# A gated mix of linear attention and a Fourier transform: x's rest rows stored by SyncE, forms stored in halves, x rings of four, low parts ahead of evictions, PE in the text's order

## The chip, the cores and the metric

The kernel runs on one core of one Trainium2 chip. The metric is the device time of one execution in microseconds. Before the change it is 793.74 us, the median of three runs (793.55 to 794.37).

A core has five engines that run their own instruction streams: PE (TensorE, matrix products, with its weight loads as PEld), DVE (VectorE), ACT (ScalarE), POOL (GpSimd) and SP (SyncE, which only issues DMAs here). Sixteen DMA engines move data between DRAM and the on-chip memory. Matrix products write to eight banks of an accumulator memory, from where DVE and ACT read them.

## The reference

```
x = A_x                                     # 2048 rows of 576
g = sigmoid((x * gate_w).sum(-1))           # one gate a row
# a: linear attention, 32 heads of 18
q, k, v = split(x @ wqkv)
pq, pk = phi(q), phi(k)                     # phi(t) = (t + 1 if t > 0 else exp(t)) + 1e-6
kv = pk^T v ; z = pk.sum(rows)              # head by head
a = (pq kv / (pq z + 1e-6)) @ wo
# b: real part of a 2-D Fourier transform, with the matrices given
b = seq_re @ (x @ hid_re^T) - seq_im @ (x @ hid_im^T)
out = g * a + (1 - g) * b
```

Everything is float32. The kernel keeps that precision by splitting each factor of a product into a high part (rounded to the type that PE takes) and a low part (what rounding left), and multiplying high by high, high by low and low by high: three matmuls for one. The high part is made by ACT (`hi_of`, L163), the low part by a subtraction on DVE (`lo_of`, L173).

## The kernel before, in words

The text runs through these stages. From the first k tiles on, ACT and DVE run in the order of the text (`pace`, L168), SP does so throughout (L199); PE's and POOL's order is set by the compiler's scheduler.

1. **k** (L508): for 16 tiles of 128 rows, two halves of 288 columns of k are computed and go through phi into `acc` and `pk`. The transposed x tiles are loaded by SP through a ring of three buffers (`xs_ring`, `load_next`, L240), split by `split_next` (L246).
2. **kv** (L583): 20 steps (five chunks of x's columns times four groups of tiles) form x^T pk; with wv this gives kv. The steps also load wv, wq and wo, and sum z.
3. **q** (L754 to L777): 16 tiles (`q_tile`, L637) give phi(q) in `acc[i]`, and the gate. `build_m` folds kv and wo into one matrix; `normalise` (L653) divides by pq z in parts, called as `go(norms)`.
4. **out** (L1055): each tile is transposed on PE (`transposed`, L681), multiplied by that matrix, scaled by the gate and stored to DRAM (`att`).
5. **hidden run 1** (`Hidden.run`, L849): x @ hid_re^T by a seven-product scheme of the Strassen kind, for eight pairs of row blocks, `p` = 0 to 7. Each product is seven matmuls: six on 512 of the columns and one on the rest rows, which are 32 x 3 rows of all forms in one tile.
6. **sequence 1** (`sequence`, L961): seq_re times the result, again with seven products, in 8 rows of output (`j`) times 4 batches (`b`); each row's seven banks are evicted by DVE (L1020 to L1038) and mixed with `att` (`mix`, L1010) into `mid`.
7. **hidden run 2** and **sequence 2**: the same with hid_im and seq_im, from `mid` to `out`.

For 5 to 7 the operands are prepared earlier as *forms*. A `Left` part (L333) loads quarters of x into SBUF, makes the sums of quarters (`make`, L352), splits them, and stores the seven forms to DRAM (`xm`, 1792 KB for a pair of blocks). Parts 2 to 6 are made during the k and kv stages, one piece a call of `left_part` (L376), which goes on to the next part when one is at its end: pieces are what stands between two `yield`s. The part of x's rest rows (`k` = `NP`) lies at `ACC_AT`, on the memory of `acc[0]` to `acc[6]`, and is stored to `xr` by six DMAs of POOL (L372), whose target is 4 x 32 rows of 3584 bytes. `right` (L382) does the same for the hidden matrices (`wm`).

In a hidden run `load_x` loads two of a pair's seven forms at a time, `load_pair` all in four DMAs, `load_rest` the rest rows (336 KB) and `load_w` one matrix form. `follow` and `follow_rest` (L852) say which pair's loads are issued during and after which pair's products. `Layout` (L89) says which memory they take.

In a sequence, `Matrix.load` fetches batches of seq (`craw`) and `make` (L942) adds forms in three pieces; the third piece first calls `tick()`, which issues the low parts that wait in `pending`, and then makes the high part. At the end of a row that third piece comes only after the first two additions of the eviction (L1022).

Of the kernel before, what the change touches and what calls it, by code (L numbers as in the profile page):

```python
# [8 lines left out]
F = mybir.dt.float32  # L9
# [66 lines left out]

LAY_Q = dict(xs=(-256, 4864, 9984), hi=(15104, 20864), lo=(26688, 31296))

# [10 lines left out]
class Layout:  # L89
# [23 lines left out]
    def rest(self, p):  # L113
        if p == 2 or p == 1 and not self.swap:
            return T_AT + (4 * TPAIR + 7 * XF if p == 2 else 60416)
        return WF_AT + 4 * WF if p % 2 else SLOT_AT + 14 * XF + 3 * WF
# [6 lines left out]
def kernel(  # L123
# [209 lines left out]
    class Left:  # L333
# [18 lines left out]
        def make(self):  # L352

            r, c = self.f[:, :, 1], self.c
            add(r[:, 0], r[:, 1], r[:, 6])
            add(r[:, 4], r[:, 2], r[:, 6], ALU.subtract)
            yield
            add(r[:, 3], r[:, 0], r[:, 2], ALU.subtract)
            add(r[:, 6], r[:, 5], r[:, 3], ALU.subtract)
            yield  # L360
            hi_of(c[:, :4, 0], r[:, :4])
            hi_of(c[:, 4:, 0], r[:, 4:])
            yield
            lo_of(c[:, :4, 1], r[:, :4], c[:, :4, 0])
            yield
            lo_of(c[:, 4:, 1], r[:, 4:], c[:, 4:, 0])
            if self.k < NP:
                nc.gpsimd.dma_start(out=xforms[self.k], in_=c.bitcast(F))
                return
            for j in range(6):  # L370
                k, g = j // 2, j % 2
                nc.gpsimd.dma_start(out=xrest[g, :, k], in_=self.plain.bitcast(F)[:, g, k // 2])  # L372

# [8 lines left out]
    def right(src, rest, order):  # L382
# [10 lines left out]
        def piece(k, start):  # L393

            c = load(k, start)
            r = c.bitcast(F)[:, :, 1]
            yield
            add(r[:, 3], r[:, 5], r[:, 0], ALU.subtract)
            add(r[:, 5], r[:, 2], r[:, 5], ALU.subtract)
            yield  # L400
            add(r[:, 4], r[:, 2], r[:, 3], ALU.subtract)
            add(r[:, 6], r[:, 4], r[:, 1], ALU.subtract)
            yield
            hi_of(c[:, :, 0], r)
            yield
            if k < 2:
                lo_of(c[:, :4, 1], r[:, :4], c[:, :4, 0])
                yield
                lo_of(c[:, 4:, 1], r[:, 4:], c[:, 4:, 0])
                nc.gpsimd.dma_start(out=main[:, :, k], in_=c.bitcast(F))  # L410
            else:
                rows = slice(32, 64)
                lo_of(c[rows, :, 0], r[rows], c[rows, :, 0])
                yield
                nc.gpsimd.dma_start(out=last, in_=c.bitcast(F)[:, :, 0])
# [92 lines left out]
    for i in range(2, NT):  # L508
# [13 lines left out]
        if 8 <= i < 12:  # L522
            xg_load()
        load_next()
        for k, j in enumerate((2, 3, 9, 13)):
# [224 lines left out]
    def m_row(h, j):  # L750
        return mhi[:, j, half(h)] if j <= KC else mlo[:, j - 5, half(h)]

    wr_forms, wr_pieces = right(wr, wr_rest, ((0, T_AT + 60416), (1, T_AT + 76544),
                                              (2, T_AT + 60416)))  # L754
    q_tile(0)
    wo_split.pop(0)()
# [9 lines left out]
    for i in range(4, NT):  # L766
# [3 lines left out]
        for k, j, n in ((0, 4, 2), (0, 5, 1), (0, 6, 2), (1, 4, 1), (1, 7, 2), (1, 8, 1),  # L770
                        (1, 11, 2), (2, 9, 1), (2, 12, 2), (2, 13, 1), (2, 14, 2)):
            if i == j:
                go(wr_pieces[k], n)
        if i in (5, 8, 13, 14, 15):
            go(norms)
        if i in (9, 10):
            split_m(i - 9)  # L777
# [29 lines left out]
    class Hidden:  # L807
# [41 lines left out]
        def run(self, m):  # L849
            rest = None  # L850

            follow, follow_rest = {0: 4, 2: 6, 3: 5, 5: 7}, {0: 4, 1: 3, 3: 5, 4: 6, 5: 7}  # L852
            self.load_pair(3)
            for p in range(NP):
                fs = Factors(T_AT + p * TPAIR)
                factors.append(fs)
                t = fs.raw
                p3, p2, e = (at(y_ring.next(), [P, HALF], F, "y") for _ in range(3))
                be, bx, bg, bf = (bank()[:, :HALF] for _ in range(4))
# [101 lines left out]
    def sequence(m, g, src, dst, last=None, between=None):  # L961
        late, held, stores = [], [], []
        for n in range(NP * NB):
# [21 lines left out]
            if n == 1:  # L985
                while backlog:
                    backlog.pop(0)()
            end = last is not None and j == NP - 1
            held.append((b, c))
# [28 lines left out]

            nc.scalar.activation(c11, ps[1], AF.Copy)
            add(c12, ps[6], c11, ALU.subtract)  # L1020
            add(c11, ps[2], c11)
# [25 lines left out]
    hidden = Hidden(wr_forms, Layout(0))  # L1047
    nxt = transposed(0)
    made = {}
# [5 lines left out]
    for i in range(NT):  # L1055
# [8 lines left out]
        nc.gpsimd.dma_start(out=att[i], in_=acc[i])  # L1064
        go(norms, 2)
        for k, n in plan.get(i, ()):
            go(made[k], n)
# [7 lines left out]
        if i == 7:  # L1075
            hidden.load_rest(0)
        for k, j in enumerate((9, 10, 13, 15, 2, 3, 4)):
            if i == j:
                hidden.load_w(k)
# [15 lines left out]
    def late(n):  # L1095
# [16 lines left out]
        if n == NP * NB - 1:  # L1112
            second.load_w(5)
            second.load_w(6)
            for k in (2, 4, 6):
                second.load_x(1, k)
            second.load_pair(2)
            second.load_rest(2)

    first.run(mr)  # L1120
    sequence(mr, gate_n, att, mid, between=late)
# [91 lines left out]
```

## Time and profile before

| | us |
|---|---|
| median of three runs (range) | 793.74 (793.55 to 794.37) |
| the profiled execution's own time | 789.25 |
| its span, first to last instruction | 787.5 |
| mean granted clock of PE | 0.979 |

The costliest groups of the page, with busy time, mean duration in ns, and the idle time just before them:

```profile
L997 PE MATMUL bank<-fh,c 128*128 128x288 f32 x1792 | 357.2, 295 | 4.6 <-DVE c L173 4.5
...
L163 ACT ACTIVATE c<-craw 128x1792 fp32r<-128x1792 f32 (+1 forms) x84 | 121.2, 1447 | 196.1 <-DVE craw L183 156.4
...
L193 PE MATMUL bank<-wd,xs 128*128 128x288 f32 (+1 forms) x896 | 128.0, 303 | 31.2 <-DVE acc L327 24.3
...
L173 DVE TENSOR_TENSOR c<-craw,c 128x1792 fp32r<-128x1792 f32 (+4 forms) x86 | 142.0, 1653 | 10.1 <-ACT c L163 10.0
...
L846 PE MATMUL bank<-wf,xf 128*128 128x288 f32 x588 | 90.0, 300 | 3.3 <-DMA xf<-xm 1.8
```

A line of the profile names the line of the kernel, the engine, the operation, and the tiles as output<-inputs. L997 is the sequences' matmul, L846 that of the hidden runs, L193 that of k, q and out. `<-` after the bar names what ended most of the idle time. Times in windows and timelines are us from the first instruction of the span.

### The profile page before, as it was taken

Reading aid. Unit: us, or ns where it says so; the run is one execution under the profiler, and the core shown is the slowest. Engines: PE = TensorE matmul, PEld = TensorE weight load, DVE = VectorE, ACT = ScalarE, POOL = GpSimd, SP = SyncE. Lnnn points to the kernel's source line nnn. Section 1 sums busy time; section 2 is a strip of 40 time slices with the busy share of each in tenths; the row PEclk is TensorE's granted clock in tenths of the full one; section 3 lists DMA queues with packets and bytes.
Section 4 is the critical chain, followed back from the end, with each engine's and each line's share of the span. In section 5 each row is a group of like instructions: output and inputs, shape, how many; then the busy total and the mean of one; then the engine's idle time right before and its main releaser. Section 6 shows DMA issues by size and latency. Waiting matters only on the chain.

```text
span 787.5 us, 13817 instructions
## 1 busy us (share of the span) xinstructions
PE 734.8 (93%) x5428; PEld 724.3 (92%) x5428; DVE 599.0 (76%) x993; ACT 332.6 (42%) x518; POOL 54.4 (7%) x92
## 2 busy tenths in 40 slices
PE   7999999339989999999999999999989999999997
PEld 7999999339979999999999999999889999999997
DVE  5769876037898894689889799983678888987775
ACT  6878435227763444344333333320343532332231
POOL 0111210005102121000000000000000000000000
PEclk9999999859999999999999999999999999999999
DMA  4476886216665589955447656868966344454441
GB/s 159 140 258 227 318 269 203 83 28 208 211 205 196 203 287 343 357 171 191 136 127 259 198 187 209 281 211 323 361 239 221 111 141 143 136 169 141 129 148 61
DMA packets 53348, 157.22 MB, mean 200 GB/s; under 512 B 7396, under 2 KB 11940, under 8 KB 52260
## 3 DMA queue, kind: packets, MB, share of 16 engines
q1 hardware_dynamic: 43620, 114.52, 44.2%
q0 software_dynamic: 9376, 41.41, 14.9%
q8 instruction: 43, 0.70, 0.4%
q10 hardware_dynamic: 288, 0.41, 0.1%
q14 instruction: 21, 0.17, 0.1%
HBM read 113.44 MB, written 41.39 MB: 197 GB/s over the span
## 4 chain that ended last, share of the span: by engine, by line
PE 58%; DMA 21%; DVE 9%; issue 7%; ACT 3%; POOL 1%; SPq 0%; DVEq 0%; ACTq 0%; POOLq 0%
PE bank L997 33%; PE bank L193 15%; DMA xf<-xm 7%; PE bank L592 6%; PE bank L846 4%; DMA wm<-wb 3%; DVE c L173 3%; DMA xraw<-in_xa_dram 2%; DMA xr<-xr 2%; DMA craw<-in_xg_dram 2%; DVE craw L183 1%; DVE ys L183 1%; DMA xr<-xb 1%; DVE wb L173 1%; DMA wraw<-in_wo_dram 1%
## 5 line engine op out<-in xcount | busy, mean ns | idle before, releaser
L997 PE MATMUL bank<-fh,c 128*128 128x288 f32 x1792 | 357.2, 295 | 4.6 <-DVE c L173 4.5
L997 PEld LDWEIGHTS bank<-fh,c 128*128 128x128 f32 x1792 | 286.3, 188 | 6.3 <-DVE c L173 5.5
L997 PE MATMUL bank<-fl,c 128*128 128x288 f32 x896 | 253.7, 294 | 0.0
L163 ACT ACTIVATE c<-craw 128x1792 fp32r<-128x1792 f32 (+1 forms) x84 | 121.2, 1447 | 196.1 <-DVE craw L183 156.4
L997 PEld LDWEIGHTS bank<-fl,c 128*128 128x128 f32 x896 | 168.6, 188 | 0.0
L193 PE MATMUL bank<-wd,xs 128*128 128x288 f32 (+1 forms) x896 | 128.0, 303 | 31.2 <-DVE acc L327 24.3
L193 PEld LDWEIGHTS bank<-wd,xs 128*128 128x128 f32 x896 | 123.7, 194 | 34.3 <-DVE acc L327 24.6
L173 DVE TENSOR_TENSOR c<-craw,c 128x1792 fp32r<-128x1792 f32 (+4 forms) x86 | 142.0, 1653 | 10.1 <-ACT c L163 10.0
L183 DVE TENSOR_TENSOR craw<-craw 128x256 f32<-128x256 f32 (+1 forms) x192 | 98.0, 512 | 6.6 <-DMA craw<-in_cr_dram 1.5
L846 PE MATMUL bank<-wf,xf 128*128 128x288 f32 x588 | 90.0, 300 | 3.3 <-DMA xf<-xm 1.8
L846 PEld LDWEIGHTS bank<-wf,xf 128*128 128x128 f32 x588 | 82.8, 191 | 5.5 <-issue 2.6
L193 PE MATMUL bank<-mw,qs 128*128 128x288 f32 x448 | 65.0, 302 | 1.6 <-ACT qs L163 1.5
L193 PEld LDWEIGHTS bank<-mw,qs 128*128 128x128 f32 x448 | 61.4, 192 | 2.5 <-ACT qs L163 1.8
L592 PE MATMUL bank<-pk,c 128*128 128x288 f32 x448 | 61.8, 296 | 1.7 <-ACT c L163 1.7
L183 DVE TENSOR_TENSOR ys<-bank,ys 128x288 f32<-128x288 f32 x63 | 28.8, 458 | 44.8 <-PE bank L997 37.1
L592 PEld LDWEIGHTS bank<-pk,c 128*128 128x128 f32 x448 | 59.7, 188 | 2.7 <-ACT c L163 2.3
L327 DVE SCALAR_TENSOR_TENSOR acc<-bank,e 128x288 f32<-128x288 f32 x64 | 28.3, 454 | 41.2 <-DMA xr<-xb 27.0
L173 DVE TENSOR_TENSOR fl<-fl,fh 128x864 fp32r<-128x864 f32 (+1 forms) x32 | 34.2, 1093 | 11.2 <-ACT fh L163 9.9
L325 ACT ACTIVATE e<-bank 128x288 f32<-128x288 f32 x64 | 25.6, 400 | 33.3 <-DVE acc L327 24.4
L163 ACT ACTIVATE fh<-fl 128x864 fp32r<-128x864 f32 (+1 forms) x32 | 29.9, 953 | 15.2 <-DVE fl L183 15.2
L173 DVE TENSOR_TENSOR xs<-xraw,xs 128x640 fp32r<-128x640 f32 (+2 forms) x33 | 26.5, 803 | 11.6 <-ACT xs L163 11.5
L1062 ACT ACTIVATE acc<-bank,gate 128x288 f32<-128x288 f32 x32 | 16.0, 501 | 40.1 <-PE bank L193 39.9
(102 smaller groups left out, 618.0 us busy)
## 6 DMA issues: line engine op xcount, KB each, us to landing
xf<-xm SPq DMA_DIRECT2D x42, 512.0 KB, 9.2
craw<-in_cr_dram SPq DMA_DIRECT2D x32, 512.0 KB, 4.0
craw<-in_ci_dram SPq DMA_DIRECT2D x32, 512.0 KB, 3.7
xm<-xb POOLq DMA_DIRECT2D x8, 1792.0 KB, 7.7
xraw<-in_xa_dram SPq DMA_DIRECT2D x31, 320.0 KB, 4.1
wm<-wb POOLq DMA_DIRECT2D x4, 2016.0 KB, 8.6
wf<-wm SPq DMA_DIRECT2D x14, 576.0 KB, 5.4
xr<-xr SPq DMA_DIRECT2D x16, 336.0 KB, 6.1
```

The costliest lines, as they stand in the source:

```text
L163: return nc.scalar.activation(dst, src, AF.Copy, bias=bias)
L173: nc.vector.tensor_tensor(out=dst, in0=src, in1=hi, op=ALU.subtract)
L183: nc.vector.tensor_tensor(out=dst, in0=a, in1=b, op=op)
L193: nc.tensor.matmul(ps, a, b, start=(n == 0), stop=(n == len(pairs) - 1))
L325: nc.scalar.activation(e, ps, AF.Relu, scale=-1.0)
L327: nc.vector.scalar_tensor_tensor(dst, ps, 0.0, e, op0=ALU.max, op1=ALU.add)
L592: nc.tensor.matmul(ps[h][:, :HALF], t[:, a, k], pk[s][:, b, half(h)], start=(s == 0 and n == 0), stop=(s == NT - 1 and n == len(passes) - 1))
L846: nc.tensor.matmul(ps, a, b, start=(start and n == 0), stop=(n == len(ops) - 1), skip_group_check=True)
L997: nc.tensor.matmul(ps[q], c[x][:, l, k], factors[p](y, f), start=(p == 0 and i == 0), stop=(p == NP - 1 and i == 2))
L1062: done.append(nc.scalar.activation(acc[i][:, half(h)], ps[:, :HALF], AF.Copy, scale=gate[:, i:i + 1]))
```

## The change

1. The six stores of x's rest rows are issued by SP, in a piece of their own after the part's last low part.
2. A form is stored in two DMAs, forms 0 to 3 when their low part is made and forms 4 to 6 after theirs (`Left` and `right`); `Left.make` yields after each half, so a part has one more piece.
3. The x ring has four buffers. In the q stage the fourth lies elsewhere; one load more is issued ahead.
4. The pieces of the third `wr` part, the norm parts and the first transposition of the out stage take other places in the q stage; three `load_w` come two tiles later.
5. In the hidden runs the rest rows of pair 3 have memory of their own and are loaded first; `follow` and `follow_rest` are reordered; in run 2 the first pair's three temporaries lie elsewhere; `second.load_rest(2)` comes before the loads of x.
6. In a sequence, `tick()` comes right after the first copy of an eviction; two of the low parts of `backlog` are issued in batch 2 after the adds of the next batch.
7. From the first hidden run on PE too runs in the order of the text.

```diff
@@ Layout.rest
-            if p == 2 or p == 1 and not self.swap:
-                return T_AT + (4 * TPAIR + 7 * XF if p == 2 else 60416)
+            if p == 2:
+                return T_AT + 4 * TPAIR + 7 * XF
+            if p == 3:
+                return T_AT + (NP - 2) * TPAIR + TPAIR // 2
+            if p == 1 and not self.swap:
+                return T_AT + 60416
@@ Left.make
-            lo_of(c[:, :4, 1], r[:, :4], c[:, :4, 0])
-            yield
-            lo_of(c[:, 4:, 1], r[:, 4:], c[:, 4:, 0])
-            if self.k < NP:
-                nc.gpsimd.dma_start(out=xforms[self.k], in_=c.bitcast(F))
-                return
-            for j in range(6):
+            for fs in (slice(0, 4), slice(4, 7)):
+                lo_of(c[:, fs, 1], r[:, fs], c[:, fs, 0])
+                if self.k < NP:
+                    nc.gpsimd.dma_start(out=xforms[self.k][:, fs], in_=c.bitcast(F)[:, fs])
+                yield
+            for j in range(0 if self.k < NP else 6):
                 k, g = j // 2, j % 2
-                nc.gpsimd.dma_start(out=xrest[g, :, k], in_=self.plain.bitcast(F)[:, g, k // 2])
+                nc.sync.dma_start(out=xrest[g, :, k], in_=self.plain.bitcast(F)[:, g, k // 2])
@@ right, piece
-                lo_of(c[:, :4, 1], r[:, :4], c[:, :4, 0])
-                yield
-                lo_of(c[:, 4:, 1], r[:, 4:], c[:, 4:, 0])
-                nc.gpsimd.dma_start(out=main[:, :, k], in_=c.bitcast(F))
+                for fs in (slice(0, 4), slice(4, 7)):
+                    lo_of(c[:, fs, 1], r[:, fs], c[:, fs, 0])
+                    nc.gpsimd.dma_start(out=main[:, fs, k], in_=c.bitcast(F)[:, fs])
+                    if fs.start == 0:
+                        yield
@@ k stage, and ahead of q_tile(0)
-        load_next()
+        if i < NT - 1:
+            load_next()
+        if i == 2:
+            load_next()
...
+    xs_ring.at[3] = T_AT + 105664
+    load_next()
     q_tile(0)
@@ q stage
-                        (1, 11, 2), (2, 9, 1), (2, 12, 2), (2, 13, 1), (2, 14, 2)):
+                        (1, 11, 2), (2, 9, 1), (2, 13, 2), (2, 14, 1)):
...
-        if i in (5, 8, 13, 14, 15):
+        if i in (5, 8, 11, 12, 13):
             go(norms)
+        if i == NT - 3:
+            nxt = transposed(0)
@@ Hidden.run
-            follow, follow_rest = {0: 4, 2: 6, 3: 5, 5: 7}, {0: 4, 1: 3, 3: 5, 4: 6, 5: 7}
+            follow, follow_rest = {0: 4, 2: 5, 3: 6, 5: 7}, {0: 4, 1: 5, 4: 6, 5: 7}
+            self.load_rest(3)
             self.load_pair(3)
...
-                p3, p2, e = (at(y_ring.next(), [P, HALF], F, "y") for _ in range(3))
+                ys = (y_ring.next() for _ in range(3))
+                if p == 0 and self.lay.swap:
+                    o = self.lay.rest(3) + XR
+                    ys = range(o, o + 3 * HALF * 4, HALF * 4)
+                p3, p2, e = (at(o, [P, HALF], F, "y") for o in ys)
@@ sequence
                 while backlog:
                     backlog.pop(0)()
+                rest_lows += pending[-2:]
+                del pending[-2:]
+            elif n == 2:
+                for f in rest_lows:
+                    f()
...
             nc.scalar.activation(c11, ps[1], AF.Copy)
+            tick()
             add(c12, ps[6], c11, ALU.subtract)
@@ out stage
+        if i == 0:
+            go(wr_pieces[2], 2)
...
-        for k, j in enumerate((9, 10, 13, 15, 2, 3, 4)):
+        for k, j in enumerate((9, 10, 13, 15, 4, 5, 6)):
             if i == j:
                 hidden.load_w(k)
@@ late, and ahead of first.run
             second.load_w(6)
+            second.load_rest(2)
             for k in (2, 4, 6):
                 second.load_x(1, k)
             second.load_pair(2)
-            second.load_rest(2)
-
+
+    paced.enter_context(tc.manual_schedule(engines={mybir.EngineType.PE}))
     first.run(mr)
```

More of the change, by code (lines that the diff above doesn't have):

```diff
@@ L74 @@
 QH = HALF, HALF + 2
-LAY_Q = dict(xs=(-256, 4864, 9984), hi=(15104, 20864), lo=(26688, 31296))
+LAY_Q = dict(xs=(-256, 4864, 9984, 43776), hi=(15104, 20864), lo=(26688, 31296))
 PRODUCTS = {1: (4, 0), 6: (2, 4), 2: (6, 1), 5: (1, 3), 7: (0, 5), 3: (3, 2), 4: (5, 6)}
@@ L961, in sequence @@
     def sequence(m, g, src, dst, last=None, between=None):
-        late, held, stores = [], [], []
+        late, held, stores, rest_lows = [], [], [], []
         for n in range(NP * NB):
@@ L1047 @@
     hidden = Hidden(wr_forms, Layout(0))
-    nxt = transposed(0)
     made = {}
```

## The prediction

> **What bounds the kernel now.** I read the page's first two parts first, then the waits of PE, then the timeline of the worst wait, then windows around it.
>
> ```profile
> span 787.5 us, 13817 instructions
> ...
> PE 734.8 (93%) x5428; PEld 724.3 (92%) x5428; DVE 599.0 (76%) x993; ACT 332.6 (42%) x518; POOL 54.4 (7%) x92
> ...
> PEclk9999999859999999999999999999999999999999
> ```
>
> PE is busy for 93% and no other engine comes near, so time is to be had only where PE stands still or runs at half clock. The eighth and ninth digits of the clock row show one such place. The waits of PE (total us, times, longest) name the others:
>
> ```profile
> PE bank L193 <- DVE acc L327: 24.3, 1, 24.3
> PE bank L997 <- DVE c L173: 4.5, 4, 1.4
> ...
> PE bank L846 <- DMA xr<-xr: 4.0, 3, 2.5
> PE bank L846 <- DMA xf<-xm: 1.8, 5, 1.0
> ...
> PE bank L193 <- ACT qs L163: 1.5, 1, 1.5
> PE bank L688 <- DVE acc L666: 1.4, 1, 1.4
> PE bank L193 <- ACT xs L163: 1.4, 3, 0.7
> PE bank L846 <- DVE fl L183: 1.2, 1, 1.2
> ```
>
> One wait is 24.3 of the 40 us listed. The timeline around it (start, length, engine, line; the idle time and its releaser in brackets):
>
> ```profile
> 126.92 6.70 SPq L554 DMA_DIRECT2D wraw<-in_wo_dram  x4
> ...
> 140.14 0.70 POOL L372 DMA_DIRECT2D xr<-xb  x1 [10.05 <-issue]
> ...
> 160.00 0.69 POOL L372 DMA_DIRECT2D xr<-xb  x1 [8.94 <-issue]
> 169.57 0.82 DVE L327 SCALAR_TENSOR_TENSOR acc<-bank,e 128x288 f32<-128x288 f32 x2 [26.95 <-DMA xr<-xb]
> ...
> 170.08 0.85 PE L193 MATMUL bank<-wd,xs 128*128 128x290 f32 x2 [24.33 <-DVE acc L327]
> ```
>
> The buffer of x's rest rows lies on acc. POOL issues its six stores some 10 us apart; the first write of acc (DVE, L327) waits until the sixth, issued at 160.0, has landed, and PE, out of banks, waits for DVE. How wide such a store runs is seen where the sixth is alone on the DMA engines (windows: length, busy of five engines, granted clock, DMA share, GB/s):
>
> ```profile
> 161.20:165.20 4.00, 0.00 (x0) 0.00 (x0) 0.00 (x0) 0.00 (x0) 0.00 (x0) 0.50 0.28 49
> 165.20:169.20 4.00, 0.00 (x0) 0.00 (x0) 0.00 (x0) 0.00 (x0) 0.00 (x0) 0.50 0.17 66
> 161.20:169.20 8.00, 0.00 (x0) 0.00 (x0) 0.00 (x0) 0.00 (x0) 0.00 (x0) 0.50 0.23 58
> 170.10:174.70 4.60, 4.11 (x15) 3.76 (x16) 4.43 (x13) 2.13 (x7) 0.00 (x0) 0.50 0.00 0
> ```
>
> A share of 0.23 of 16 engines is 3.7: the store keeps some four engines busy, at 58 GB/s. The last row is the bill that comes after the wait: 4.6 us at half clock, 2.3 us lost.
>
> **The change part by part.**
>
> *Stores of the rest rows.* The six issues leave POOL for SP; source, destination and the 3.5 KB stretches stay what they were.
>
> ```profile
> xm<-xb POOLq DMA_DIRECT2D x8, 1792.0 KB, 7.7
> ...
> mid<-row SPq DMA_DIRECT2D x16, 288.0 KB, 4.2
> ...
> xr<-xb POOLq DMA_DIRECT2D x6, 448.0 KB, 10.2
> ```
>
> When do they start? `make` now yields once more for each left part, so `left_part` takes five calls for every part where the last call of one used to be the first of the next. Counted through the 12 calls of the k loop and the 20 steps after it, the rest part is made in steps 13 to 17 and stored in step 18, not in step 12. In SP's order that is behind the loads of wo, whose last issue ends at 126.92 + 6.70 = 133.6. So the stores start 26 us later than POOL's first, and gain only if they run more than that much faster. SP's queue does not wait for each to land, so the 10 us pacing goes. What it leaves is the stream: 6 x 448 KB = 2.75 MB. Bounds: at SP's best rate (the 364 GB/s of a window shown below) 7.6 us; at the 49 GB/s of the first window 56 us. I take the row of this very transfer, with its shape: four engines. The first store takes its 8.0 us. The slow start of a single store (49 GB/s at a share of 0.28, 4.5 engines, 11 GB/s each) gives way to 66 GB/s at 0.17, 2.7 engines, 24 GB/s each; four engines with work always queued then move 97 GB/s, 4.7 us a store. The end is 133.6 + 1.2 (issue at 160.0, data by 161.2) + 8.0 + 5 x 4.7 + 0.3 (169.2 to 169.57) = 166.6 against 169.57: **2.9 us gained**, and the half clock stays. Behind the stores on SP wait the loads of x tiles 3 and on; tiles 0 to 2 are in SBUF, so PE has work when acc opens. Step 12's load of wq now waits for the store of form 6, made four steps later than before; I put the delay of c and wv behind it at 2 us (half a form's 7.7 us, less the lead of c), hidden as long as the stores end late.
>
> The Trainium skill, "DMA: Bandwidth & Descriptors", section "Why a DMA increments its semaphore by 16 and not by 1", says that a transfer runs on as many engines as the largest number up to 16 that divides its slowest dimension, whichever engine issues it. It speaks against this change: the slowest dimension is 4 here, and the share of 0.23 agrees for POOL; no row shows SP with it. By that rule the sum stays as it is. The same page, section "Bandwidth", gives 341 GB/s for a load of 1 MB over 128 partitions; by that the six would be over in an estimated 8 us, which is the first rival below.
>
> *Rings of four, q's end.* The three waits on xs (1.4 us in all) go: each x tile is loaded one tile earlier, and SP has idle time there. At the end of the q stage:
>
> ```profile
> 229.11 2.25 DVE L173 TENSOR_TENSOR wb<-wb 32x2016 fp32r<-32x2016 f32 x1
> ...
> 231.40:235.50 4.10, 1.12 (x6) 0.67 (x5) 3.93 (x10) 2.22 (x7) 0.78 (x1) 1.00 0.74 239
> 236.10:239.50 3.40, 3.30 (x15) 3.19 (x14) 3.33 (x8) 0.00 (x0) 0.00 (x0) 0.50 0.28 58
> ```
>
> DVE is full (3.93 of 4.10) while PE stands, and then PE runs 3.4 us at half clock. The change takes that low part (2.25 us) behind the first out tile, moves three norm parts two tiles ahead and tile 0's transposes to tile 13, where PE has two tiles of work split. That removes 1.5 + 1.4 + 1.7 (half of 3.4) = **4.6 us**, with 1.4 for the ring **6.0**. What is late next is the second out tile's low part, behind 2.25 us more on DVE; it has two tiles' time.
>
> *Forms in halves.* Twelve more POOL issues; POOL is busy for 7%: nothing. In the first hidden run the rest of pair 3 now goes into memory that the last form leaves, so SP stands at its start until that form is stored. The old order had that wait a little later:
>
> ```profile
> SPq L938 <- DMA xm<-xb: 5.8, 1, 5.8
> ```
>
> Pairs 0 to 2 are there by then, so PE has 20 us of cover. This run's small waits for xf and xr (0.6 and 0.4 of the 1.8 and 4.0) go: **1.0**.
>
> *Low parts ahead of evictions.*
>
> ```profile
> 371.07 4.56 DVE L173 TENSOR_TENSOR fl<-fl,fh 128x864 fp32r<-128x864 f32 x4
> ...
> 380.21 1.02 DVE L183 TENSOR_TENSOR ys<-bank,ys 128x288 f32<-128x288 f32 x2 [1.55 <-ACT ys L1019]
> 381.15 2.02 DVE L173 TENSOR_TENSOR c<-craw,c 128x1792 fp32r<-128x1792 f32 x1
> ```
>
> DVE stands for 1.55 us until the bank is copied, evicts, and only then makes the low part for which PE waits. With `tick()` before the first add it starts 1.0 to 2.5 us sooner, and every one of the four waits is at most 1.4: 4.5 us go. Banks come free 2 us later; the next row needs the second of them after two products of 6 matmuls, 1.6 us. Against it, two of the four low parts of 4.56 us go behind the next batch's adds, and PE needs the last of them some 0.3 us early in each sequence: 0.6. **3.9 us.**
>
> *Second hidden run, PE in text order.*
>
> ```profile
> 543.05 0.41 ACT L872 ACTIVATE y<-bank 128x288 f32<-128x288 f32 x1 [6.38 <-DVE row L1013]
> ...
> 540.00:560.00 20.00, 18.66 (x138) 18.05 (x137) 12.26 (x25) 6.04 (x12) 0.00 (x0) 1.00 0.98 364
> 560.00:580.00 20.00, 16.12 (x103) 15.03 (x102) 9.69 (x20) 4.14 (x8) 0.00 (x0) 0.91 1.04 359
> ...
> 574.00:577.50 3.50, 3.40 (x14) 3.40 (x15) 2.31 (x4) 1.16 (x3) 0.00 (x0) 0.51 1.04 407
> ...
> 560.01 0.32 SPq L822 DMA_DIRECT2D xr<-xr  x1
> ...
> 569.93 0.80 PE L846 MATMUL bank<-wf,xr 96*128 96x288 f32 x4 [1.09 <-DMA xr<-xr]
> ```
>
> The first product's copy no longer shares a buffer with the sequence's mixes, so the wait of 1.2 goes. For the rest the DMA engines are the wall (shares 0.98 and 1.04). A pair is 49 matmuls, 49 x 18.66 / 138 = 6.6 us of PE, and 1792 + 336 KB = 2.18 MB, 6.0 us of DMA: pairs come hardly faster than they are used. Rests 2 and 3 move forward and no more bytes move. Gone are the waits on xr (1.1 + 2.5) and xf (1.2, what the first run leaves) and half of 3.5 us of clock: 7.7 with the 1.2. New: rest 4 stays behind pair 4 and gets rest 3's 0.9 us in front of it, so it comes at about 570.8, while PE in text order wants it in pair 4's first product, at 540.5 + 4 x 6.6 + 0.9 = 567.8, plus the 0.4 that pair 1 waits for its second load behind rest 2: 2.6 + 0.4 + 0.4 for pair 3's first load. **7.7 - 3.4 = 4.3 us.** Here a gap of 2.6 us might halve the clock again, as the two gaps at 231.4 did (PE busy 1.12 of 4.10). The Trainium skill, "TensorE: Matmul & The Clock Gate", Part 1, puts the window at about 3.4 us, so 2.6 us would leave the clock whole; the trace's 3.0 us in two gaps did not. By the page the term is 4.3, with a halving 2.6; I keep 4.3.
>
> **Sum.** 2.9 + 6.0 + 1.0 + 3.9 + 4.3 = 18.1 us off the profiled span, 769.4 of 787.5. That execution took 789.25 us beside a median of 793.74, so I carry the difference, not the level: 793.74 - 18.1 = **775.6**.
>
> **The rivals.**
> - *SP spreads the stores* as it does its 128-row ones: 7.6 us of stream, acc opens at about 142.7, before PE runs dry at 145.75 (170.08 - 24.33). Then 24.3 + 2.3 go instead of 2.9, less 2 us of the delays in steps 12 to 17, now uncovered: 793.7 - 15.2 - 26.6 + 2 = 754. For it: SP's `mid` stores land in 4.2 us. Against it: the same shape took four engines.
> - *The stores end later than POOL's* (the slower side). If the four engines hamper each other all the time as in the first window, 49 GB/s, the stream takes 56 us and acc opens at 191: 21 us more wait, 793.7 - 15.2 + 21.4 = 800. At the 58 GB/s of a whole store it is 182 and 791. It turns slower than before at a stream of 50 us, 55 GB/s. For it: six starts in six looked alike at 10 us each. Against it: queued engines don't all start together again.
> - *Text order and late loads take back the hidden runs' and sequences' gains*: without 1.0, 3.9 and 4.3 the time is 785. For it: DMA is full there. Against it: the bytes are the same and the rests come sooner.
>
> **How the numbers follow.** Forecast 0.60; spread 0.17; late stores 0.13, half of it slower than before; gains taken back 0.10. Forecast alone: 766 to 783. The range takes in 754 and 58 GB/s: 752 to 791. A measurement here tells about 0.2% from no change: faster by more 0.90, within 0.03, slower 0.07.
>
> **What would show it.** The stores: their issue times on SP (133 to 136), a DMA share near 0.25 after it, and the wait of DVE at L327 ending near 167 (143 or 182 for the rivals). The others: no wait of L688 and L193 near 231, waits of L997 on c under 0.6 in all, no L872 wait on row, and one wait on xr of 2 to 3 us in the second run. I am wrong if SP's issue itself blocks on its four rings and holds back the x tiles, or if acc waits for fewer than all six.

## The result, and the profile after

The changed kernel takes 770.96 us (median of four runs, 767.95 to 771.47) against 794.06 us before (793.55 to 798.15): a ratio of 0.969, 95% interval 0.965 to 0.9731. It is faster, inside the range of 752 to 791, and 4.6 us below the forecast of 775.6. Between the two profiled executions (789.25 and 771.09) lie 18.2 us, by their spans 18.1; by the medians it is 23.1, since the profiled execution of before lay 4.8 us under its median. That sum of 18.1 is what the prediction gave, but not by its terms.

Page of after (compare the span, PE's busy time and the clock row):

```profile
span 769.4 us, 13840 instructions
...
PE 732.4 (95%) x5428; PEld 727.6 (95%) x5428; DVE 600.7 (78%) x993; ACT 336.0 (44%) x518; POOL 56.7 (7%) x98
...
PEclk9999999859999999999999999999999999999999
```

The dent in the clock row is still in the eighth and ninth digits. Waits of PE, after (total us, times, longest):

```profile
PE bank L197 <- DVE acc L331: 19.4, 1, 19.4
...
PE bank L857 <- ACT y L888: 2.4, 2, 1.3
PE bank L857 <- DMA xr<-xr: 2.3, 1, 2.3
PE bank L197 <- ACT zs L167: 1.9, 1, 1.9
PE bank L857 <- DVE fl L187: 1.5, 3, 0.8
```

L197 was L193, L331 was L327, L857 was L846. The wait on acc shrank by 4.9 us. The waits on c, qs, acc L666, xf and on the x tiles of the ring are gone. Two lines are new: y, the copy of a product's bank in a hidden run, and zs, the tile from which z is summed. Waits on fl, a hidden run's result before its low part is made, come three times in place of once.

Where the 18.1 us came from is seen when both executions are cut at the same points: acc's first write after the stall, the first out tile, the first hidden product, the first product of run 2. First before, then after (length of the stretch, PE busy with its matmuls, granted clock, DMA share, GB/s):

```profile
0.00:169.57 169.57, 138.28 (x1008) 0.94 0.60 195
169.57:232.95 63.38, 60.12 (x431) 0.96 0.55 181
232.95:304.04 71.09, 69.53 (x518) 0.98 0.67 234
304.04:540.53 236.49, 232.22 (x1738) 1.00 0.66 224
540.53:787.50 246.97, 234.60 (x1738) 0.99 0.53 174
```

```profile
0.00:164.84 164.84, 138.83 (x1008) 0.94 0.60 202
164.84:226.18 61.34, 60.33 (x430) 0.94 0.57 183
226.18:293.52 67.34, 67.34 (x521) 1.00 0.76 258
293.52:526.97 233.45, 231.92 (x1739) 1.00 0.66 223
526.97:769.40 242.43, 234.01 (x1738) 0.99 0.54 178
```

Acc opens 4.7 us sooner, and this alone counts of all that lies ahead of it, since PE stands there for whatever else comes early or late. Then the stretches gain 2.0 (the rest of q), 3.75 (out), 3.0 (run and sequence 1) and 4.5 us (run and sequence 2): 18.1 with the 4.7, but for rounding. In the out stage PE is now busy for all of its 67.34 us.

### The profile page after: what moved, and what is told of

It is laid out like the page before. It is cut to its first block, busy times and chain, and to the rows that moved or that the text cites. A ratio compares the mean times of both kernels' runs of the same rounds, so it can differ in the third digit from the quotient of the medians.

```text
span 769.4 us, 13840 instructions
## 1 busy us (share of the span) xinstructions
PE 732.4 (95%) x5428; PEld 727.6 (95%) x5428; DVE 600.7 (78%) x993; ACT 336.0 (44%) x518; POOL 56.7 (7%) x98
## 4 chain that ended last, share of the span: by engine, by line
PE 71%; DMA 10%; DVE 2%; SPq 2%; issue 1%; ACT 0%; DVEq 0%; ACTq 0%
PE bank L1018 46%; PE bank L197 16%; PE bank L857 6%; DMA xf<-xm 4%; DMA xr<-xr 2%; DMA xraw<-in_xa_dram 2%; DMA mid<-row 1%; PE bank L695 1%; PE bank L599 1%; SPq L375 1%; DMA wraw<-in_wv_dram 1%; DMA xm<-xb 1%; SPq L247 1%; DVE fl L177 1%; DVE fl L187 0%
## 5 line engine op out<-in xcount | busy, mean ns | idle before, releaser
L1018 PE MATMUL bank<-fl,c 128*128 128x288 f32 x896 | 264.4, 295 | 0.0
L197 PE MATMUL bank<-wd,xs 128*128 128x288 f32 (+1 forms) x896 | 128.1, 305 | 24.7 <-DVE acc L331 19.4
L197 PEld LDWEIGHTS bank<-wd,xs 128*128 128x128 f32 x896 | 125.2, 196 | 26.2 <-DVE acc L331 19.6
L857 PE MATMUL bank<-wf,xf 128*128 128x288 f32 x588 | 93.9, 300 | 4.1 <-ACT y L888 2.4
L857 PEld LDWEIGHTS bank<-wf,xf 128*128 128x128 f32 x588 | 84.8, 191 | 6.0 <-ACT y L888 3.0
L197 PE MATMUL bank<-mw,qs 128*128 128x288 f32 x448 | 63.3, 298 | 0.0
L331 DVE SCALAR_TENSOR_TENSOR acc<-bank,e 128x288 f32<-128x288 f32 x64 | 28.3, 454 | 43.4 <-DMA xraw<-in_xa_dram 23.1
L599 PEld LDWEIGHTS bank<-pk,c 128*128 128x128 f32 x448 | 61.3, 193 | 0.1
L197 PEld LDWEIGHTS bank<-mw,qs 128*128 128x128 f32 x448 | 60.0, 188 | 0.2 <-DVE qs L177 0.2
L857 PE MATMUL bank<-wf,xr 96*128 96x288 f32 x112 | 33.7, 301 | 2.3 <-DMA xr<-xr 2.3
```

Of the source, the lines that this page charges most:

```text
L197: nc.tensor.matmul(ps, a, b, start=(n == 0), stop=(n == len(pairs) - 1))
L331: nc.vector.scalar_tensor_tensor(dst, ps, 0.0, e, op0=ALU.max, op1=ALU.add)
L599: nc.tensor.matmul(ps[h][:, :HALF], t[:, a, k], pk[s][:, b, half(h)], start=(s == 0 and n == 0), stop=(s == NT - 1 and n == len(passes) - 1))
L857: nc.tensor.matmul(ps, a, b, start=(start and n == 0), stop=(n == len(ops) - 1), skip_group_check=True)
L1018: nc.tensor.matmul(ps[q], c[x][:, l, k], factors[p](y, f), start=(p == 0 and i == 0), stop=(p == NP - 1 and i == 2))
```

## The experiments

The line numbers of a run are its own kernel's; they differ by a few from those of after. The times of before beside the runs had medians of 792.0 to 794.3 us.

### What the stores of the rest rows cost: number of engines

The timeline of after: SP's issues, then the first write of acc; PE, which waits for it, goes on at 165.35, after 19.42 us:

```profile
132.92 15.37 SPq L375 DMA_DIRECT2D xr<-xb  x6
```

```profile
164.84 0.82 DVE L331 SCALAR_TENSOR_TENSOR acc<-bank,e 128x288 f32<-128x288 f32 x2 [23.15 <-DMA xraw<-in_xa_dram]
```

Six issues take 15.37 us, where the kernel `relaid` below issues six stores of the same bytes in 5.21: SP itself is held up. The wait of DVE ended with several releases, and the profile names a load of x that stood behind the stores. The windows show that the stores were still running (`pool18` below, where those loads don't stand behind the stores, settles that the stores hold acc):

```profile
136.00:144.00 8.00, 8.00 (x64) 8.00 (x63) 3.65 (x7) 3.84 (x11) 0.00 (x0) 1.00 0.25 90
...
160.00:164.00 4.00, 0.00 (x0) 0.00 (x0) 0.00 (x0) 0.00 (x0) 0.00 (x0) 0.50 0.26 104
```

A share of 0.25 is four engines of 16, at 136 us and still at 160, with 90 to 104 GB/s. To see whether the four engines are the cause, each store was cut into four of 32 rows (kernel `stores32`):

```diff
-                nc.sync.dma_start(out=xrest[g, :, k], in_=self.plain.bitcast(F)[:, g, k // 2])
+                for b in range(4):
+                    nc.sync.dma_start(out=xrest[g, b, k],
+                                      in_=self.plain.bitcast(F)[32 * b:32 * b + 32, g, k // 2])
```

> The changed kernel with each of the six stores of rest rows cut into four stores of 32 rows, 24 in all, in the same place on SyncE. Theory (a store whose slowest dimension is 4 runs on four DMA engines, and this stream holds acc): 24 issues at the 0.48 us between two of SP's other issues (303.03, 303.50) are 11.5 us, so the last is issued near 145 and lands near 148; acc opens there in place of 164.8, the stall of 19.4 us shrinks to 0 to 3 us and the half clock behind it goes too (some 3 us): 748 to 756 us. Rival (the bytes or the late start set the end, not the number of engines): acc opens near 165 as before, 768 to 773 us.

Measured: 752.57 us (ratio to before 0.9471, 0.9407 to 0.9535). In a second kernel the rest rows lie in DRAM as 128 rows one behind the other, and their loads come in three pieces (`relaid`):

```diff
-    xrest = scratch([2, 4, 3, 32, 7, P], "xr")
+    xrest = scratch([2, 3, P, 7, P], "xr")
...
-                nc.sync.dma_start(out=xrest[g, :, k], in_=self.plain.bitcast(F)[:, g, k // 2])
+                nc.sync.dma_start(out=xrest[g, k], in_=self.plain.bitcast(F)[:, g, k // 2])
...
-            nc.sync.dma_start(out=self.rest[p].bitcast(F)[:96],
-                              in_=xrest[p // 4, p % 4].rearrange("j r f n -> (j r) f n"))
+            j = p % 4 * 32
+            for k in range(3):
+                nc.sync.dma_start(out=self.rest[p].bitcast(F)[32 * k:32 * k + 32],
+                                  in_=xrest[p // 4, k, j:j + 32])
```

> The changed kernel with the rest rows laid out in DRAM as 128 rows one behind the other, so that each of the six stores has a slowest dimension of 128, and each load of them in three pieces of 32 rows. Theory (four engines bind the stores): 2.75 MB at the 364 GB/s that SP's loads reach are 7.6 us, acc opens near 143, before PE runs dry at 145.9: 746 to 752 us, unless the 32 added issues on SP in the hidden runs (0.33 us each) make rests late. Rival (start and bytes bind): 768 to 773 us.

Measured: 749.39 us (0.9439, 0.9384 to 0.9493). PE's wait on acc is 1.7 us in `stores32`. In `relaid`, the window that was shown of after:

```profile
136.00:144.00 8.00, 8.00 (x65) 8.00 (x64) 3.91 (x10) 4.31 (x11) 0.00 (x0) 1.00 0.79 291
```

The same bytes from the same place run at a share of 0.79 and 291 GB/s, and with `relaid` PE has no wait on acc at all. So the stall was the four engines, and with all 16 the late start is no harm: the theory held. The Trainium skill, "DMA: Bandwidth & Descriptors", section "Why a DMA increments its semaphore by 16 and not by 1", has a transfer use the largest number of engines up to 16 that divides the slowest dimension of both its sides. The trace agrees for SP too, with a share of 0.25 where that dimension is 4 in DRAM, and 0.79 where it is 128.

### What they cost: issuer and place

The six stores of the changed kernel go back to POOL, in the new place (`pool18`):

```diff
-                nc.sync.dma_start(out=xrest[g, :, k], in_=self.plain.bitcast(F)[:, g, k // 2])
+                nc.gpsimd.dma_start(out=xrest[g, :, k], in_=self.plain.bitcast(F)[:, g, k // 2])
```

> The changed kernel with the six stores issued by GpSimd, as before the change, but in the new place (step 18). Theory (the issuer matters: GpSimd paces the six some 10 us apart, and the move to SyncE pays for a start 26 us later): the sixth is issued near 185 and lands near 194, PE stands for some 49 us in place of 19.4: about 800 us, 795 to 805. Rival (pacing comes from the four engines and not from the issuer): the stores go out 5 us apart as on SyncE, 768 to 775 us.

Measured: 795.41 us (1.0023, 0.9986 to 1.0059), at the low end of the theory. Its timeline of POOL, first and last of the six, and DVE's first write of acc:

```profile
127.17 0.75 POOL L375 DMA_DIRECT2D xr<-xb  x1 [15.58 <-ACT wd L167]
```

```profile
178.06 0.70 POOL L375 DMA_DIRECT2D xr<-xb  x1 [8.98 <-issue]
```

```profile
187.70 0.82 DVE L331 SCALAR_TENSOR_TENSOR acc<-bank,e 128x288 f32<-128x288 f32 x2 [47.54 <-DMA xr<-xb]
```

From the first issue to the sixth are five steps in 50.9 us, 10.2 each, against some 5 for a store on SP, and PE's wait on acc is 44.0 us. Here SP is free and issues the first loads of x from 138.8 us on, and acc opens only at 187.7, released by a store: so acc waits for the stores, not for the loads of x. Why POOL takes 10 us for each was not tried. All else of the change is in this kernel, and is eaten up by the later place. The reverse is the kernel before with nothing but the queue changed (`sp12`):

```diff
-                nc.gpsimd.dma_start(out=xrest[g, :, k], in_=self.plain.bitcast(F)[:, g, k // 2])
+                nc.sync.dma_start(out=xrest[g, :, k], in_=self.plain.bitcast(F)[:, g, k // 2])
```

> The kernel before the change, with nothing changed but the six stores' queue: SyncE in place of GpSimd, in the old place (step 12). Theory (the stores' later place costs what their faster queue gives): from 107 us on the stores take 5 us each, acc opens near 140, the stall of 24.3 us and its half clock (2.3 us) go, and loads of xg, wv, wq and wo that stand behind the stores on SyncE come up to 15 us late, which costs PE some of it back: 768 to 778 us. Rival (SyncE, blocked by the stores, starves PE in the kv stage for as long as the stores take): 783 to 794 us.

Measured: 792.84 us (0.9986, 0.9953 to 1.0019): no gain, as the rival had it. The waits of PE, the timeline of SP and that of ACT:

```profile
PE bank L193 <- ACT zs L163: 24.9, 1, 24.9
```

```profile
115.39 14.88 SPq L372 DMA_DIRECT2D xr<-xb  x6
```

```profile
150.15 0.63 ACT L163 ACTIVATE c<-craw 128x512 fp32r<-128x512 f32 x1 [29.21 <-DMA craw<-in_xg_dram]
```

The 24.3 us on acc are gone, and 24.9 us on zs stand in their place: SP is held by the stores, the load of a chunk of c behind them lands late, and ACT, in the text's order, stands at that chunk with the high part of zs behind it. So the queue alone gains nothing, and the new place with POOL's queue loses what all else of the change gains. SP's stores pay where nothing that PE needs soon is queued behind them, and that is step 18.

### The sequences: low parts or PE's order

`notick` takes back the low parts ahead of evictions; `noorder` takes back PE's text order; `neither` takes back both:

```diff
-                rest_lows += pending[-2:]
-                del pending[-2:]
-            elif n == 2:
-                for f in rest_lows:
-                    f()
...
             nc.scalar.activation(c11, ps[1], AF.Copy)
-            tick()
```

```diff
-    paced.enter_context(tc.manual_schedule(engines={mybir.EngineType.PE}))
     first.run(mr)
```

> The changed kernel without the low parts ahead of the evictions in the sequences (no call of tick behind the copy of bank 1, and the two low parts kept for the third batch back in the second), all else as changed, PE's text order too. Theory (these low parts are what PE waited for): the four waits of PE on c, up to 1.4 us each, come back, 4 to 6 us: 775 to 777 us. Rival (it was PE's text order that removed them): no waits on c, 769 to 772 us.

> The changed kernel with PE's instructions from the first hidden run on left to the scheduler again, all else as changed. Theory (the text's order is worth nothing by itself, since the same data comes at the same time): 769 to 773 us. Rivals: the text's order carries part of the sequences' and runs' gain, 774 to 778 us; or it costs the wait for rest 4 of pair 4, which a free order fills with other products, 766 to 769 us.

Measured: 771.58 us (0.9712, 0.9676 to 0.9747) and 769.26 us (0.9682, 0.9647 to 0.9717). Neither is told from after (0.969) within these intervals, and neither has a wait on c. So the prediction's reason for this term, that the low part is made too late, is not enough: in `notick` it ends 3.4 us after the copy of bank 1 begins, as in before, and PE does not wait.

> The changed kernel with both taken back: the low parts ahead of the evictions, and PE in the text's order. Each alone left the sequences without a wait on c. Theory (either one suffices, since each puts more of PE's work between the copy of bank 1 and the next batch's low part than before the change): with neither, the waits on c come back, 4 to 6 us in all: 774 to 778 us. Rival (something else of the change, the loads or the runs, removed them): no waits on c, 768 to 772 us.

Measured: 773.22 us (0.9749, 0.971 to 0.9788), a little under the range of the theory. The time decides little, since it also holds a wait of 3.6 us on fl in the second hidden run; the waits on c decide. These are its waits and the timelines of ACT, DVE and PE:

```profile
PE bank L1013 <- DVE c L177: 3.1, 3, 1.4
```

```profile
368.02 0.41 ACT L1035 ACTIVATE ys<-bank 128x288 f32<-128x288 f32 x1 [0.76 <-PE bank L1013]
```

```profile
369.41 2.02 DVE L177 TENSOR_TENSOR c<-craw,c 128x1792 fp32r<-128x1792 f32 x1
```

```profile
371.48 0.53 PE L1013 MATMUL bank<-fh,c 128*128 128x288 f32 x2 [1.40 <-DVE c L177]
```

The waits on c are back, 3.1 of 4.5 us. The low part ends 3.4 us after the copy of bank 1 begins (369.41 + 2.02 - 368.02), and PE came to it after 2.1 us (371.48 - 1.40 - 368.02). In `notick` the same low part also ends 3.4 us after the copy, and PE isn't there yet:

```profile
365.61 0.39 ACT L1035 ACTIVATE ys<-bank 128x288 f32<-128x288 f32 x1
```

```profile
366.97 2.02 DVE L177 TENSOR_TENSOR c<-craw,c 128x1792 fp32r<-128x1792 f32 x1
```

In the text's order bank 1's product comes first and six more products of six matmuls follow it: 36 matmuls, which start every 0.13 us in this stage, are some 4.8 us. So the low part can be made sooner, or PE can come to it later; one of the two is enough. That the scheduler's order keeps less behind bank 1 is read from these times.

### The hidden runs' loads, and q's end

`oldruns` has the hidden runs' orders, the memory of rest 3, the place of the second run's rest 2 and that of its first three copies as before; of its edit only the first part is shown:

```diff
-            follow, follow_rest = {0: 4, 2: 5, 3: 6, 5: 7}, {0: 4, 1: 5, 4: 6, 5: 7}
-            self.load_rest(3)
+            follow, follow_rest = {0: 4, 2: 6, 3: 5, 5: 7}, {0: 4, 1: 3, 3: 5, 4: 6, 5: 7}
```

> The changed kernel with the hidden runs' loads as before the change (orders of the following pairs and rests, place of rest 3, second run's rest 2 last, its first three copies in the ring), all else as changed. Theory (the two runs together gained 1.9 us by the trace: 2.5 in the second, 0.6 lost in the first): 772 to 774 us, the waits on xr and xf of the second run come back and PE's two waits on y (1.10 and 1.30 us), which are behind the load of the first matrix batch, get shorter. Rival (the forecast's 5.3 us are right, and the waits on y come from elsewhere): 775 to 778 us with the waits on y as they are.

Measured: 778.1 us (0.9789, 0.9753 to 0.9826). Its wait on rests:

```profile
PE bank L855 <- DMA xr<-xr: 13.3, 3, 8.9
```

The time is at the top of the rival's range, the waits on y are gone, where the theory had them shorter, and the reason is neither's: PE in the text's order stands at a late rest for up to 8.9 us. Before the change the same orders cost 4.0 us on xr, with PE free to take other products. Beside the text's order the new load orders are worth 7 us. That they would be worth less under a free order is read from before's row; it was not run. `oldqend` has the end of q as before:

```diff
-        if i in (5, 8, 11, 12, 13):
+        if i in (5, 8, 13, 14, 15):
             go(norms)
-        if i == NT - 3:
-            nxt = transposed(0)
```

The pieces of wr, the weight loads and tile 0's transposes go back with it.

> The changed kernel with the end of the q stage as before the change (norm parts, pieces of wr, tile 0's transposes and the weight loads in their old places), all else as changed, the ring of four too. Theory (these moves are the 6.9 us that the trace shows between 200 and 240 us): 776 to 779 us, with waits of 1.4 to 1.5 us on the first transposes and the first out tile and a half clock behind them. Rival (the ring of four or the earlier stores made q's end lighter): 770 to 773 us.

Measured: 777.35 us (0.9779, 0.9742 to 0.9815), 6.4 us over after, with the waits on qs (1.5 us) and on acc (1.0 us) back. The rest of q and the out stage, cut at the same points as above:

```profile
163.60:226.52 62.92, 60.39 (x431) 0.94 0.56 179
226.52:297.17 70.65, 69.55 (x518) 0.98 0.70 246
```

That is 1.6 and 3.3 us longer than in after, 4.9 in all, and the stretches behind it are alike. These moves carry q's end.

### The new waits

Two places in after's timeline hold the new waits. The first is at zs. The lines show SP's wait before a load of wq, for the store of a form, and that load's issue, 4.9 us after SP's last issue of c; ACT's wait for the chunk of c behind it; PE's wait for ACT; and the four matmuls of zs in all, to 131.6:

```profile
SPq L298 <- DMA xm<-xb: 4.7, 1, 4.7
```

```profile
117.15 0.38 SPq L298 DMA_DIRECT2D wraw<-in_wq_dram  x1
```

```profile
123.86 0.63 ACT L167 ACTIVATE c<-craw 128x512 fp32r<-128x512 f32 x1 [4.41 <-DMA craw<-in_xg_dram]
```

```profile
126.61 0.40 PE L197 MATMUL bank<-zs,ones 128*128 128x288 f32 x1 [1.93 <-ACT zs L167]
```

```profile
L197 PE MATMUL bank<-zs,ones x4: 293/356/399, 126.6 to 131.6; 128*128 128x288 f32 x4
```

The second is in run 2. The lines show DVE's wait at the first matrix batch, and what PE stands at:

```profile
559.60 0.69 DVE L187 TENSOR_TENSOR craw<-craw 128x512 f32<-128x512 f32 x1 [6.53 <-DMA craw<-in_ci_dram]
```

```profile
557.74 0.40 PE L857 MATMUL bank<-wf,xr 96*128 96x288 f32 x1 [2.34 <-DMA xr<-xr]
```

```profile
562.70 1.07 PE L857 MATMUL bank<-wf,xf 128*128 128x288 f32 x6 [1.30 <-ACT y L888]
```

The clock in the stretch behind each was this (the granted clock is the third number from the right):

```profile
128.10:131.50 3.40, 3.40 (x17) 3.40 (x16) 2.97 (x6) 2.04 (x6) 0.00 (x0) 0.50 0.02 8
558.20:561.60 3.40, 3.20 (x14) 2.85 (x12) 1.96 (x5) 0.17 (x1) 0.00 (x0) 0.50 1.00 311
```

Each of the two gaps, of 2.3 us in all, is followed by 3.4 us at half clock. The next kernels try to take them away, on the base of `relaid`. `relaid-wq13` issues wq's second half a step later:

```diff
-            if step in (9, 12):
+            if step in (9, 13):
```

> The kernel with the rest rows laid out as 128 rows, and the load of the second half of wq in step 13 in place of 12. Theory (SyncE stands at this load until the last pair's form is stored, and the loads of c and wv behind it come late): the waits on zs (1.12 and 0.39 us) and the half clock behind them (1.7 us) go: 749.4 - 3 = 745 to 747 us. Rival (zs is late for another reason, or wq then comes late): 749 to 751 us.

Measured: 746.03 us (0.9412, 0.9377 to 0.9446), no wait on zs, mean clock 0.998 against 0.992 of `relaid`: the theory held. SP's wait for the form's store is 0.8 us here. Its timeline of SP and its four matmuls of zs show more:

```profile
122.41 5.13 SPq L561 DMA_DIRECT2D wraw<-in_wo_dram  x4
127.76 5.25 SPq L375 DMA_DIRECT2D xr<-xb  x6
```

```profile
L197 PE MATMUL bank<-zs,ones x4: 294/295/296, 124.0 to 126.5; 128*128 128x288 f32 x4
```

The stores go out at 127.76, where after has 132.92. The fourth load of wo takes the memory of zs (`wo_at`, K_AT + 3 * XD), so it waits until PE has read zs, and the stores stand behind it on SP: 1.3 us from the last matmul of zs to the first store in both kernels. So in after the late zs also made the stores late, by some 5 us. That acc would have opened as much sooner there follows from the order on SP; it was not run with stores on four engines.

`relaid-runs` moves the add of the first batch (`first`) from pair 3's fourth product to pair 4's fifth, its later steps a pair later too, and rest 4 ahead of two of pair 4's four pieces:

```diff
-                        if p == 3:
-                            first = m.make()
-                        if p == 3:
-                            next(first)
...
+                        if p == 4:
+                            first = m.make()
+                            next(first)
...
-                    if p in follow and k in (1, 3, 5, 6):
+                    if p in follow and k in ((1, 3, 5, 6) if p else (1, 3)):
...
                     self.load_rest(follow_rest[p])
+                if p == 0:
+                    self.load_x(4, 4)
+                    self.load_x(4, 6)
```

> The kernel with the rest rows laid out as 128 rows, and two edits in the hidden runs: the first step of the first matrix batch (an add of DVE that waits for its load) behind pair 4's fifth product in place of pair 3's fourth, and rest 4's load ahead of the last two pieces of pair 4. Theory (DVE, in order, stands at that add and holds the adds, the high part and the copy that PE needs next; rest 4 comes behind four pieces): of the run before, the waits on y (2.25 and 1.15 us), on fl (0.4, 0.3), the wait on xr of 3.07 us and two half clocks of 1.7 us go, less about 1 us that the bytes cost elsewhere: 749.4 - 9 = 739 to 742 us. Rival (the DMA engines are full there, so the waits only move to other loads): 745 to 750 us.

Measured: 747.28 us (0.9418, 0.938 to 0.9455), the rival's time. The waits on y are gone, so DVE's stand at the batch made them. But the waits on rests grew from 3.1 us in `relaid` to 4.3, the longest now some 15 us later in the run. With the DMA engines at a share of 1.0 around that wait, the load that went ahead pushed another back. The last kernel keeps the first edit and wq's, and leaves rest 4 where the change put it (`all-three`):

> Rest rows laid out as 128 rows, wq's second half in step 13, and the first matrix batch's add behind pair 4's fifth product (rest 4's load left where the change has it, since moving it ahead only moved the wait to rest 6). Theory (the three gains lie in different stages and add up): no wait on acc, zs or y; of the 2.7 us of the longest wait on y in the run before and the one of 0.8 us in the first hidden run some 3 to 4 us go: 746 - 3.5 = 741 to 744 us. Rival (the second hidden run is bound by its loads, so that a gap that goes there comes back as a wait on xr or xf): 745 to 748 us.

Measured: 740.74 us (739.45 to 741.68), a ratio to before of 0.9325, 0.9299 to 0.9351, a little better than the theory. The engines' row of its page and its longest waits but for one of 3.9 us at the start, when nothing is loaded yet (its clock row has no dent):

```profile
PE 726.3 (98%) x5428; PEld 723.1 (98%) x5428; DVE 601.6 (81%) x993; ACT 336.0 (45%) x518; POOL 56.7 (8%) x98
```

```profile
PE bank L859 <- DMA xr<-xr: 3.2, 1, 3.2
PE bank L859 <- DMA wf<-wm: 1.4, 1, 1.4
```

These two lie in the second hidden run, and behind the longer PE runs at a granted clock of 0.50 for 3.4 us, from 529.9 to 533.3. So what is left to gain in this order of work is an estimated 3.2 + 1.4 + 1.7, some 6 us.

## Why the prediction was right, and where its terms were not

- **Stores of the rest rows** (2.9 us). Right in mechanism: four engines, issues from 132.9 (forecast 133.6), acc open at 164.84 (166.6). The term was 4.7. Of the 1.8 us more, 0.7 is the start; the rest is the stream, forecast with its ends at 33.0 us from the first issue to acc (1.2 + 8.0 + 23.5 + 0.3), measured at 31.9. Of what would have made it wrong, one thing was half met: SP did block (15.37 us for six issues), but the x tiles behind it were not needed before acc opened. `sp12` shows what that costs where something is.
- **The delay of c and wv** (2 us, hidden). This step failed. The prediction saw that wq's load would stand in step 12 until form 6 is stored, and took the stall as cover for what comes late. The wait on zs and its half clock are indeed covered by the stall. But zs also releases the load of wo in front of the stores, which the prediction left out: what is late there moves the stall's end. The forecast start was taken from the loads of wo in before; it came out because before's own zs was about as late as after's, and that is luck, as before's view of that tile shows:

```profile
L193 PE MATMUL bank<-zs,ones x4: 294/295/296, 128.5 to 131.0; 128*128 128x288 f32 x4
```

- **Rings of four and q's end** (1.4 + 4.6 = 6.0). Right: 2.0 + 3.75 = 5.8. The part of the ring in the k stage, two of the three waits (0.7 us), should not have been counted, since it lies ahead of the stall; q's end gave a little more than its 4.6, by `oldqend`'s two stretches 4.9.
- **The hidden runs** (1.0 + 4.3). Mis-sized. The waits of the first run did not go: on xf and xr they did, but 1.1 us on y and 0.3 on fl came, 1.4 for 1.0. In the second run, the wait for rest 4 came as forecast (2.34 for 2.6) but halved the clock, which the prediction named and did not count. And a wait came that it did not see: DVE, in order, stands at the first batch of the matrix (6.53 us in run 2), and y with it. `relaid-runs` and `all-three`, where the waits on y are gone from both runs, show that this is the cause. Why the batch itself is late was not taken apart further; its load stands behind rests and forms on a full DMA.
- **Low parts ahead of evictions** (3.9). The waits on c went, all 4.5 us, but the reason given is only half of it: PE's text order does the same by itself. Runs and sequences together gave 7.6 us (236.49 - 233.45 and 246.97 - 242.43) of the 9.2 forecast. With 4.5 for the waits on c, 3.1 of the 5.3 are left for the runs; counted by PE's waits inside them, 7.0 us before and 6.1 after, it is only 0.9. Which of the two is nearer stays open.
- **The rivals.** "SP spreads the stores" did not happen here, and its price was near: 754 forecast for it, 752.6 and 749.4 measured once the stores were given the shape. "The stores end later than POOL's" did not happen on SP: four engines moved 90 to 104 GB/s, not 49 to 58. With POOL in the same place the stores did end later, at a time of 795.4, but by POOL's pace of 10 us. "Text order and late loads take back the gains" came true for a small part, 1.6 of the 9.2 us; `oldruns` shows how much more it would have been with the old orders.
- **The sum.** That 18.1 was forecast and 18.1 came by the spans is luck, since errors cancel: the stores gave 1.8 more, the runs and sequences 1.6 less, the ring and q's end 0.2 less. The 5 us by which the medians differ further were in before's median and not in its profiled execution; before's runs beside the experiments went from 786.4 to 800.1 us, and what spreads them was not tried.

## What to carry to other kernels

Give a DMA a slowest dimension that is a multiple of 16, as the 32 and 128 here, before moving it to another queue: here the shape was worth 22 us (771.0 to 749.4), and the move of queue alone nothing. Before a slow store goes to a queue that also loads, list what is issued behind it and who waits for that. And where an engine is put in the text's order, every load in that text has to be in the order of need, for a late one can no longer be passed by.

## What the runs showed that was not expected

SP is held while its stores run on four engines: six issues took 15.37 us, half of the 31.9 us until acc opened, where 24 stores of 32 rows took 12.35 us and six of 128 rows 5.21. And gaps of 1.93 + 0.40 and of 2.34 us were enough for 3.4 us at half clock. The Trainium skill, "TensorE: Matmul & The Clock Gate", Part 1, has the clock fall after an idle window of some 3.4 us; in these two places the measurement differs, since PE stood for less. The length of a gap alone does not decide it either: in `relaid` gaps of 1.12 + 0.39 us were followed by 3.4 us at half clock, and in `relaid-wq13` single gaps of 1.92 and 2.04 us were not. What decides was not found.
